# Attention followed by a soft mixture of experts, on one core: five rotating sigmoid buffers, V in three single-buffered tiles, 50 weight units loaded beside attention, and another warm-up

## The chip, the cores and the metric

The kernel runs on one core of a Trainium2 chip. The time is the device time of one execution in microseconds (us); less is better. Before the change the median of three runs is 392.14 us (391.18 to 392.22).

## What is computed

Sigmoid attention (8 batches, 12 heads, 448 tokens, heads of 64), whose output, as 3584 rows of 768, goes through a soft mixture of 8 experts with 4 slots each:

```python
scores = scale * np.matmul(q, k.transpose(0, 1, 3, 2)) - np.log(S)
attn = 1.0 / (1.0 + np.exp(-scores))
x = np.matmul(attn, v)            # then to (N, D) rows
logits = x @ phi
d = softmax(logits, axis=0); slot_input = d.T @ x
slot_out[e] = np.maximum(slot_input[e] @ w1[e], 0.0) @ w2[e]
out = softmax(logits, axis=1) @ slot_out
```

All of it is in float32. The weights w1 and w2 are 48 MB together, more than fits beside the rest.

## The kernel before

**Queues.** The order of the instructions on each engine's queue is the order of the program text; the tile framework adds the waits. All transfers are issued by SP (SyncE), one after the other, and an issue whose destination is not yet free holds up all those behind it.

**Attention.** Two heads make a pair, two pairs (pa, pb) a group, three groups a batch; the loop runs over 24 groups n. A pair's 448 keys are three blocks of 128 and a rest of 64; the rests of the two pairs of a group are worked together as the "middle" block. In a group TensorE does: `qk_full(pa)` and `qk_full(pb)` (L171: scores of three blocks each, in three products with the operands split in two parts by `split`, L150 and L152), `av_full(pa)` and `av_full(pb)` (L189, attention times V), the product with phi for the group before (`logits`, L218; between the two AV halves in the first group of a batch, "edge"), in the second group of a batch ("after") the slot products of the batch before (`slot_mm`, L312, which read the tile y), then `qk_mid(n + 1)` (L182) and `av_mid(n)` (L198). Each block's scores lie in one of four double banks of PSUM (b0 to b3); ScalarE turns them to attention by `sigmoid` (L161). VectorE copies the result out (`evac`, L207), transposes it into y (`turn`), splits the next q and k, adds the logits (L227, L229) and does the softmax steps. The blocks of a group (u = 0 to 5) use the tiles att0 to att4, u = 5 taking att0 again; the middle blocks use attm0 and attm1 in turn.

**Loads beside attention.** In a group SP issues the q and k of the next two pairs (`load_qk`, L135, two buffers), V of the next group (`load_v`, L142, two buffers of 448 KB), and some units of the weights. The weights are 128 units of 384 KB: 64 of w1, then 64 of w2. They go to a ring of 68 tiles: 47 (wa, N_A) that have room from the start and are filled beside attention, and 21 (wb, N_B) that lie where the pools of attention lay. `weights_of` gives 3 units a group in the first batch and then 4, 0 and 3 until N_A are loaded.

**The end of attention.** In group 23 the logits and slots of the last batch follow at once: `last_job` with its own `slot_mm`. After the loop the pools of attention (from q and k to the transposed x) are closed, and the pool wb is opened at the same address; each wb tile waits only for the tiles that lay under it. SP then issues the N_B units, and in the parts `w1_part` (L522), `w2_step` (L588) and `out_batch` (L565, L570, stores at L579) each further unit goes to a ring tile whose weights have been used.

**Start.** SP loads q and k of the first two pairs, V, the constants and phi. TensorE meanwhile runs `WARM` products of 128 x 128 by 128 on zeros (L407), then `qk_mid(0)`.

Of the kernel before, what the change touches and what calls it, by code (L numbers as in the profile page):

```python
# [9 lines left out]
F32 = mybir.dt.float32  # L10
# [6 lines left out]
B, H, S, D = 8, 12, 448, 64  # L17
DM, NSLOT, E, SPE, F = 768, 32, 8, 4, 1024
P = 128
NFULL = 3  # L20
# [4 lines left out]
NFC = F // P  # L25
HALF = DM // 2
UNIT = 768
N_A = 47
N_B = 21
N_LATE = 16  # L30
N_MIX = 4
NATT = 5
QW = 2 * S
NP = B * NPR
NG = B * NQ
WARM = 8
WN = 128
CW = 256
NBK = 4
# [8 lines left out]
def soft_moe_attention(ctx: ExitStack, tc: tile.TileContext, qk, v, phi, w1, w2, cst, out):  # L48
    nc = tc.nc
# [15 lines left out]
    acc = small.tile([P, DM], F32, name="acc")  # L65
# [11 lines left out]
    def ring_tile(dt=F32):  # L77
        n = state["ring"]
        state["ring"] = n + 1
        n %= N_A + N_B  # L80
        if n < N_A:
            return wpa.tile([P, UNIT], dt, name=f"wa{n}")
        return state["wpb"].tile([P, UNIT], dt, name=f"wb{n - N_A}")

    def load_unit():
        n = state["next"]
        if n >= len(units):
            return
        state["next"] = n + 1
        u = units[n]  # L90
        t = ring_tile()[:]
        nc.sync.dma_start(t, w1[u[1:]] if u[0] == "w1" else w2[u[1:]])
        utile[u] = t
# [22 lines left out]
    with ExitStack() as actx:  # L116
        ldq = actx.enter_context(tc.tile_pool(name="ldq", bufs=2))
        sp = actx.enter_context(tc.tile_pool(name="sp", bufs=2))
        ata = actx.enter_context(tc.tile_pool(name="ata", bufs=1))
        atb = actx.enter_context(tc.tile_pool(name="atb", bufs=1))  # L120
        lvp = actx.enter_context(tc.tile_pool(name="lvp", bufs=2))
        yp = actx.enter_context(tc.tile_pool(name="yp", bufs=1))
        xp = actx.enter_context(tc.tile_pool(name="xp", bufs=1))
        bounce = actx.enter_context(tc.tile_pool(name="bounce", bufs=2, space=bass.MemoryType.DRAM))
# [2 lines left out]
        def bank2(i):  # L127
            return ps.tile([P, 2, 512], F32, name=f"b{i}")

        qkts, vs, splits, atts, avs, xTs, ys, dts, drs = {}, {}, {}, {}, {}, {}, {}, {}, {}  # L130

        def load_qk(p):
            if p < NP:
                t = ldq.tile([P, QW], F32, name="qkt")
                nc.sync.dma_start(t[:], qk[p])  # L135
                qkts[p] = t

        def load_v(n):
            if n == NG:
                return  # L140
            vs[n] = lvp.tile([P, 2 * NFULL + 1, P], F32, name="v")
            nc.sync.dma_start(vs[n][:], v[n])  # L142

        def split(p, i, z, copy=nc.vector.tensor_copy):
            w = (S, NQK)[i]
# [11 lines left out]
                    split(p, i, z)  # L157

        def sigmoid(name, sc):
            att = (atb if name == "att0" else ata).tile([P, 2, S], F32, name=name)  # L160
            nc.scalar.activation(att[:], sc[:, :, 0:S], AF.Sigmoid, bias=nbias, scale=QSCALE)  # L161
            return att

        def qk_full(p):
            qs, ks = splits[p, 0], splits[p, 1]
            for c in range(NFULL):
                u = p % 2 * NFULL + c
                sc = bank2(u % 4)
                for z, y in ((0, 0), (0, 1), (1, 0)):
                    for h, r in enumerate(heads):  # L170
                        nc.tensor.matmul(  # L171
                            sc[:, h, 0:S], ks[r, z, c * P:(c + 1) * P], qs[r, y, :], start=(z + y == 0), stop=(z == 1))
                atts[p, c] = sigmoid(f"att{u % NATT}", sc)

        def qk_mid(n):
            if n == NG:
                return
            sc = bank2(3)
            for i, r in enumerate(heads):
                t = qkts[2 * n + i]  # L180
                for h, d in enumerate(heads):
                    nc.tensor.matmul(sc[r, h, 0:S], t[d, S + NQK:QW], t[d, 0:S], start=True, stop=True)  # L182
            atts["mid", n] = sigmoid(f"attm{n % 2}", sc)

        def av_full(p, start, stop):
            n, i = divmod(p, 2)
            for c in range(NFULL):
                for h, r in enumerate(heads):
                    nc.tensor.matmul(  # L189
                        avs["p", p][r, 0:S], vs[n][:, i * (NFULL + 1) + c, r], atts[p, c][:, h, :],  # L190
                        start=(start and c == 0), stop=(stop and c == NFULL - 1))

        def av_mid(n, flags):
            att, vt = atts["mid", n], vs[n]
            for h, d in enumerate(heads):
                for i, r in enumerate(heads):
                    start, stop = flags[i]
                    nc.tensor.matmul(avs["p", 2 * n + i][d, 0:S], vt[r, NFULL, d], att[r, h, :], start=start, stop=stop)  # L198

        def new_x(n):  # L200
            xTs[n] = xp.tile([P, 2, S], F32, name="xT", bufs=2)
# [29 lines left out]
        def logits(n, i):  # L231
            lp = bank2(i)[:, 0, :]
            logits_job(lp, (2 * n, 2 * n + 1))
            return lp
# [161 lines left out]
        def weights_of(n):  # L396
            share = 3 if n < NQ else (4, 0, 3)[n % NQ]
            return max(0, min(share, N_A - state["next"]))

        load_qk(0)  # L400
        load_qk(1)
        load_v(0)
        nc.sync.dma_start(csb[:], cst)
        nc.sync.dma_start(phi_sb, phi)
        pw = bank2(0)[:, 0, :]
        for _ in range(WARM):
            nc.tensor.matmul(pw[:, 0:WN], acc[:, 0:P], acc[:, 0:WN], start=True, stop=True)  # L407
        dmy = ata.tile([P, 2, S], F32, name="attm0")
        nc.scalar.activation(dmy[0:1, 0, 0:1], nbias[0:1, :], AF.Sigmoid)
        split(0, 0, 0)  # L410
        split(0, 1, 0, nc.scalar.copy)
# [5 lines left out]
        for n in range(NG):  # L417
            pa, pb = 2 * n, 2 * n + 1
            bp = n // NQ - 1
            edge, after, third = (n >= NQ and n % NQ == i for i in range(3))  # L420
            final = n == NG - 1
            load_qk(pa + 2)
            load_qk(pb + 2)
            if third:
                slot_evac(bp)
            if n > 0:
                evac(n - 1)
                for p in ((pa - 4, pa - 3) if third else ()) + (() if after else (pa - 2, pa - 1)):
                    turn(p)
            if after:  # L430
                softmax_r(bp)
                softmax_c(bp)
                spread(bp)
            load_v(n + 1)
            for _ in range(weights_of(n)):
                load_unit()
            if third:
                combine_c(bp)
            if edge and bp > 0 or final:
                bq = bp if final else bp - 1  # L440
                combine_d(bq, dts[bq][:, 0, 0:P])
            qk_full(pa)
            split_all(pa + 2)
            qk_full(pb)
            split_all(pb + 2)
            if final:
                avs["p", pa] = bank2(2)[:, 0, :]
                av_full(pa, True, False)
                lg = bank2(0)[:, 0, 0:P]
                nc.tensor.matmul(lg, ident, lt_all[:, B - 1], start=True, stop=False)  # L450
                logits_job(lg, [NP - 4, NP - 3], first=False, last=False)
                avs["p", pb] = bank2(3)[:, 0, :]
                av_mid(n, ((False, True), (True, False)))
                xa = xp.tile([P, 2, S], F32, name="xT", bufs=2)[:, 0, :]
                xTs["p", pa] = xa
                nc.vector.tensor_copy(xa, avs["p", pa][:, 0:S])
                turn(pa)
                av_full(pb, False, True)
                logits_job(lg, [pa], first=False, last=False)
                xb = xp.tile([P, 2, S], F32, name="xT", bufs=2)[:, 0, :]  # L460
                xTs["p", pb] = xb
                nc.scalar.copy(xb[:, 256:S], avs["p", pb][:, 256:S])
                nc.vector.tensor_copy(xb[:, 0:256], avs["p", pb][:, 0:256])
                logits_job(lg, [pb], first=False)
                turn(pb)
                break
            avs[n] = bank2(2)
            for i in range(2):
                avs["p", pa + i] = avs[n][:, i, :]
            av_full(pa, True, False)  # L470
            if edge:
                lp = logits(n - 1, 0)
                logits_add(lp, bp, False)
                softmax_a(bp)
                softmax_b(bp)
            av_full(pb, True, False)
            if n > 0 and not edge:
                lp = logits(n - 1, 3 if after else 0)
                if after:
                    combine_b(bp)  # L480
                logits_add(lp, n // NQ, n % NQ == 1)
            if after:
                slot_job(bp)
            qk_mid(n + 1)
            av_mid(n, ((False, True), (False, True)))
# [7 lines left out]
    for e in range(E):  # L493
        if e < 3:
            if e == 0:
                hacc = small.tile([P, DM], F32, name="acc")
            h = hacc[:, e * 256:(e + 1) * 256]
        elif e < 5:
            h = small.tile([P, 256], F32, name=("phit", "t1")[e - 3])[:]
        else:  # L500
            h = sb2.tile([P, 256], F32, name=f"h{e}", bufs=1)[:]
# [10 lines left out]

    for _ in range(N_B):
        load_unit()
# [151 lines left out]
```

## Time and profile before

| | |
|---|---|
| median of 3 runs | 392.14 us |
| the profiled execution | 390.38 us |
| its span, first to last instruction | 388.6 us |
| TensorE busy (matmuls) | 365.3 us, 94% |
| VectorE, ScalarE busy | 226.1 us, 187.5 us |
| moved by the DMA engines | 97.5 MB, 251 GB/s over the span |
| granted TensorE clock, mean | 0.986 |

The profile comes from one execution. The engines are PE (TensorE matmuls), PEld (its weight loads), DVE (VectorE), ACT (ScalarE), POOL (GpSimd) and SP, whose issues of transfers are called SPq. L with a number is a line of the kernel; a name such as wa or att stands for all tiles of that name. A float32 product is two records on PE. Matmuls overlap one another, so a busy PE says that products are under way, not that the array is full.

### The profile page before, as it was taken

The page shows a single profiled execution, that of the slowest core. Times are in us where ns is not written, and L with a number is a line of the kernel's source. Part 1 is how long each engine was busy: PE and PEld are TensorE (multiplying, and loading weights), DVE is VectorE, ACT ScalarE, POOL GpSimd, SP SyncE. Part 2 cuts the span into 40 slices and gives each one's busy share as a digit, 9 for nine tenths or more (in the row PEclk, how much of TensorE's full clock was granted, in tenths as well). Part 3 has the DMA queues.
Part 4 walks back from the last instruction along what each step waited for, and adds up shares of the span by engine and source line. Part 5 has one row for each costly group of instructions (what it writes and reads, how often), then busy time and mean ns, then how long its engine had stood idle before and what let it go on. Part 6 is the DMA issues. An engine that isn't in the chain of part 4 may idle for free.

```text
span 388.6 us, 9551 instructions
## 1 busy us (share of the span) xinstructions
PE 365.3 (94%) x3994; PEld 189.8 (49%) x3994; DVE 226.1 (58%) x518; ACT 187.5 (48%) x243; POOL 3.3 (1%) x13
## 2 busy tenths in 40 slices
PE   8999999999999999999999999999989989978760
PEld 7444556554555654555554455554455543224220
DVE  3655677775887677697767777776543410430250
ACT  5655676564567556566635666564531110320240
POOL 1000000000000000000000000000020000000000
PEclk9999999999999999999999999999999999999995
DMA  7766855662784567476446654323999999999997
GB/s 228 260 240 236 300 171 183 237 252 83 265 295 138 178 229 255 135 257 240 177 140 228 238 164 156 143 101 98 292 406 400 400 400 400 398 407 399 373 302 231
DMA packets 42363, 97.52 MB, mean 251 GB/s; under 512 B 4816, under 2 KB 16720, under 8 KB 42320
## 3 DMA queue, kind: packets, MB, share of 16 engines
q1 hardware_dynamic: 42320, 96.91, 70.3%
q8 instruction: 31, 0.51, 0.5%
q14 instruction: 12, 0.10, 0.1%
HBM read 85.43 MB, written 11.47 MB: 249 GB/s over the span
## 4 chain that ended last, share of the span: by engine, by line
PE 80%; DMA 14%; DVE 1%; SPq 1%; ACT 1%; issue 0%; ACTq 0%
PE b L189 29%; PE b L171 24%; DMA wa<-in_w_dram 8%; PE b L182 6%; DMA wb<-in_w_dram 6%; PE b L198 5%; PE b L312 4%; PE px L522 4%; PE b L218 3%; PE b L407 1%; PE px L565 1%; PE px L539 1%; SPq L579 1%; DMA out_dram<-wa 1%; DVE wa L570 0%
## 5 line engine op out<-in xcount | busy, mean ns | idle before, releaser
L161 ACT ACTIVATE att<-b,nbias 128x896 f32<-128x896 f32 x144 | 131.9, 1015 | 12.0 <-PE b L171 12.0
L189 PE MATMUL b<-att,v 128*64 128x448 f32 x576 | 115.3, 545 | 0.0
L171 PE MATMUL b<-qs,ks 64*128 64x448 f32 x864 | 95.9, 372 | 0.0
L171 PEld LDWEIGHTS b<-qs,ks 64*128 64x128 f32 x864 | 77.4, 184 | 26.6 <-PE b L182 11.3
L189 PEld LDWEIGHTS b<-att,v 128*64 128x64 f32 x576 | 38.5, 136 | 61.6 <-issue 50.2
L161 ACT ACTIVATE attm<-b,nbias 128x896 f32<-128x896 f32 x24 | 24.2, 1008 | 70.4 <-PE b L182 70.4
L207 DVE COPY xT<-b 128x896 f32<-128x896 f32 x23 | 25.1, 1092 | 32.7 <-PE b L198 32.7
L152 DVE TENSOR_TENSOR qs<-qkt,qs 128x448 fp32r<-128x448 f32 x48 | 30.0, 625 | 1.7
L152 DVE TENSOR_TENSOR ks<-qkt,ks 128x384 fp32r<-128x384 f32 x48 | 26.8, 558 | 1.6
L213 DVE STREAM_TRANSPOSE y<-xT 128x448 f32<-128x448 f32 x48 | 27.3, 617 | 0.4
L182 PE MATMUL b<-qkt 64*64 64x448 f32 x192 | 24.1, 570 | 0.0
L150 DVE CAST qs<-qkt 128x448 fp32r<-128x448 f32 x48 | 18.2, 380 | 8.8 <-DMA qkt<-in_qk_dram 7.7
L198 PE MATMUL b<-attm,v 64*64 64x448 f32 x192 | 22.4, 537 | 0.0
L570 DVE COPY wa<-px 96x768 f32<-96x768 f32 x13 | 12.2, 952 | 13.7 <-PE px L565 12.9
L570 ACT COPY wa<-px 128x768 f32<-128x768 f32 x13 | 10.3, 799 | 18.1 <-PE px L565 14.2
L565 PE MATMUL px<-st,lt_all 32*128 32x384 f32 (+1 forms) x128 | 16.7, 524 | 1.5 <-DVE st L601 0.7
L312 PE MATMUL b<-y,dr 32*32 32x192 f32 x896 | 17.7, 331 | 0.2 <-ACT dr L303 0.2
L218 PEld LDWEIGHTS b<-xT,phit 128*32 128x32 f32 x384 | 9.1, 109 | 17.0 <-issue 13.4
L522 PE MATMUL px<-wa,sT 128*32 128x256 f32 x282 | 16.8, 381 | 0.6 <-DVE sT L380 0.6
L150 DVE CAST ks<-qkt 128x384 fp32r<-128x384 f32 x47 | 16.6, 353 | 0.0
L218 PE MATMUL b<-xT,phit 128*32 128x96 f32 (+1 forms) x384 | 16.0, 266 | 0.2
L601 DVE COPY st<-px 128x384 f32<-128x384 f32 x2 | 1.1, 557 | 25.3 <-PE px L599 25.3
(132 smaller groups left out, 229.3 us busy)
## 6 DMA issues: line engine op xcount, KB each, us to landing
wa<-in_w_dram SPq DMA_DIRECT2D x92, 384.0 KB, 7.7
qkt<-in_qk_dram SPq DMA_DIRECT2D x48, 448.0 KB, 3.8
wb<-in_w_dram SPq DMA_DIRECT2D x36, 384.0 KB, 5.7
v<-in_v_dram SPq DMA_DIRECT2D x24, 448.0 KB, 5.7
out_dram<-wa SPq DMA_DIRECT2D x26, 192.0 KB, 3.3
out_dram<-wa SPq DMA_DIRECT2D x26, 144.0 KB, 3.3
dr<-zd SPq DMA_DIRECT2D x28, 64.0 KB, 2.0
out_dram<-wb SPq DMA_DIRECT2D x6, 192.0 KB, 5.5
```

What stands on the lines that cost most here:

```text
L150: copy(dst[:, 0, :], src)
L152: nc.vector.tensor_tensor(out=dst[:, 1, :], in0=src, in1=dst[:, 0, :].bitcast(F32), op=ALU.subtract)
L161: nc.scalar.activation(att[:], sc[:, :, 0:S], AF.Sigmoid, bias=nbias, scale=QSCALE)
L171: nc.tensor.matmul(sc[:, h, 0:S], ks[r, z, c * P:(c + 1) * P], qs[r, y, :], start=(z + y == 0), stop=(z == 1))
L182: nc.tensor.matmul(sc[r, h, 0:S], t[d, S + NQK:QW], t[d, 0:S], start=True, stop=True)
L189: nc.tensor.matmul(avs["p", p][r, 0:S], vs[n][:, i * (NFULL + 1) + c, r], atts[p, c][:, h, :], start=(start and c == 0), stop=(stop and c ...
L198: nc.tensor.matmul(avs["p", 2 * n + i][d, 0:S], vt[r, NFULL, d], att[r, h, :], start=start, stop=stop)
L207: nc.vector.tensor_copy(xTs[n][:], avs[n][:, :, 0:S])
L213: nc.vector.transpose(ys[b][:, hp, :], xTs["p", p])
L218: nc.tensor.matmul(lp[32 * j:32 * j + 32, 0:TOK[j]], phi_sb[:, p % NPR, :], xTs["p", p][:, TOF[j]:TOF[j] + TOK[j]], start=(first and m == ...
L312: nc.tensor.matmul(sl[a // 2][32 * j:32 * j + 32, a % 2, 0:NPR * BLK], drs[b][32 * a:32 * a + 32, j, c * BLK:(c + 1) * BLK], y[32 * a:32 * ...
L522: nc.tensor.matmul(ph[32 * j:32 * j + 32, uu, 0:256], sT[:, 3 * kh + kc, :], utile[("w1", e, 2 * uu + j // 2, kh)][:, kc * 256:(kc + 1) * ...
```

## The change

The seven sigmoid tiles become five, att0 to att4, each in a pool of its own. They rotate from group to group: after each middle block the list of names is permuted, so that the middle block of the next group stays where it is while the six blocks of the group use the other four. V becomes three tiles with one buffer each: v0 and v1 (192 KB, the three full blocks of either pair) and v2 (64 KB, the middle block), loaded by three transfers at different places of SP's queue. The pools are opened in another order: q and k, their split forms, v0, att4, att3, v2, att0, att1, att2, v1, then y, dr and the transposed x as before. N_A is 50 and N_B 18. The logits of an edge group go to bank 3 instead of bank 0. The warm-up is 37 products of 32 x 32 by 8 columns, on the four diagonal blocks of the array in turn, and three of the old kind.

```diff
-N_A = 47
-N_B = 21
+N_A = 50
+N_B = 18
-NATT = 5
-WARM = 8
+WARM = 3
+FILL = 37
...
-        ata = actx.enter_context(tc.tile_pool(name="ata", bufs=1))
-        atb = actx.enter_context(tc.tile_pool(name="atb", bufs=1))
-        lvp = actx.enter_context(tc.tile_pool(name="lvp", bufs=2))
+        one = {}
+        for name in ("v0", "att4", "att3", "v2", "att0", "att1", "att2", "v1"):
+            one[name] = actx.enter_context(tc.tile_pool(name=f"{name}p", bufs=1))
...
-        def load_v(n):
+        def load_v(n, part):
             if n == NG:
                 return
-            vs[n] = lvp.tile([P, 2 * NFULL + 1, P], F32, name="v")
-            nc.sync.dma_start(vs[n][:], v[n])
+            lo, hi = ((0, NFULL), (NFULL + 1, 2 * NFULL + 1), (NFULL, NFULL + 1))[part]
+            vs[n, part] = one[f"v{part}"].tile([P, hi - lo, P], F32, name=f"v{part}")
+            nc.sync.dma_start(vs[n, part][:], v[n, :, lo * P:hi * P])
...
-            att = (atb if name == "att0" else ata).tile([P, 2, S], F32, name=name)
+            att = one[name].tile([P, 2, S], F32, name=name)
...
+        homes = [f"att{i}" for i in range(5)]
...
-                atts[p, c] = sigmoid(f"att{u % NATT}", sc)
+                atts[p, c] = sigmoid(homes[u % 4], sc)
...
-            atts["mid", n] = sigmoid(f"attm{n % 2}", sc)
+            atts["mid", n] = sigmoid(homes[2], sc)
+            homes[:] = [homes[i] for i in (3, 0, 1, 4, 2)]
...
-        load_v(0)
+        load_v(0, 0)
+        load_v(0, 1)
...
+        for i in range(FILL):
+            r = slice(i % 4 * 32, i % 4 * 32 + 32)
+            nc.tensor.matmul(pw[r, 0:8], acc[r, 0:32], acc[r, 0:8], start=True, stop=True)
...
+            if third:
+                load_v(n, 1)
             load_qk(pa + 2)
             load_qk(pb + 2)
+            load_v(n, 2)
...
-            load_v(n + 1)
             for _ in range(weights_of(n)):
                 load_unit()
+            load_v(n + 1, 0)
+            if not after:
+                load_v(n + 1, 1)
...
-                lp = logits(n - 1, 0)
+                lp = logits(n - 1, 3)
```

The uses of V in `av_full` and `av_mid` follow the new tiles.

## Rows read from the trace of the kernel before

**Rows 1.** Page, part 2: busy tenths in 40 slices of 9.7 us
```profile
PE   8999999999999999999999999999989989978760
DMA  7766855662784567476446654323999999999997
```

**Rows 2.** Page, part 4: share of the chain that ended last, by line
```profile
PE b L189 29%; PE b L171 24%; DMA wa<-in_w_dram 8%; PE b L182 6%; DMA wb<-in_w_dram 6%; PE b L198 5%; PE b L312 4%; PE px L522 4%; PE b L218 3%; PE b L407 1%; PE px L565 1%; PE px L539 1%; SPq L579 1%; DMA out_dram<-wa 1%; DVE wa L570 0%
```

**Rows 3.** The chain in order of time, 268 to 292 us: start, length, what
```profile
274.75 2.41 PE b L189 x12
...
278.15 0.91 PE b L198 x8
279.06 2.43 PE b L189 x12
...
285.43 2.35 PE b L312 x93
```

**Rows 4.** Timeline of SP's issues from 264 and from 287.7 us: start, length, what
```profile
270.11 19.45 SPq L92 DMA_DIRECT2D wb<-in_w_dram  x21
...
287.80 1.75 SPq L92 DMA_DIRECT2D wb<-in_w_dram  x4
```

**Rows 5.** Busy time by stretch: its length, five engines, clock, DMA share, GB/s
```profile
271.00:272.00 1.00, 1.00 (x12) 0.81 (x10) 1.00 (x2) 0.50 (x2) 0.00 (x0) 1.00 0.71 203
...
279.00:280.00 1.00, 1.00 (x10) 0.47 (x8) 0.85 (x2) 0.00 (x0) 0.00 (x0) 1.00 1.15 283
...
288.00:289.20 1.20, 0.94 (x16) 0.29 (x8) 0.58 (x2) 0.24 (x2) 0.87 (x4) 1.00 1.03 407
270.00:289.20 19.20, 18.49 (x268) 10.07 (x260) 10.87 (x28) 10.08 (x16) 1.19 (x5) 1.00 0.90 317
289.20:362.00 72.80, 66.86 (x760) 29.32 (x760) 18.25 (x39) 10.49 (x26) 0.99 (x4) 1.00 1.04 401
```

**Rows 6.** Timeline of DVE, ACT and PE in group 3, 36 to 50 us
```profile
45.30 0.56 DVE L229 TENSOR_TENSOR lt_all<-b,lt_all 64x128 f32<-64x128 f32 x2 [0.41 <-PE b L218]
...
39.27 5.50 ACT L161 ACTIVATE att<-b,nbias 128x896 f32<-128x896 f32 x6 [0.56 <-PE b L171]
...
38.29 3.98 PE L171 MATMUL b<-qs,ks 64*128 64x448 f32 x36
42.20 2.48 PE L189 MATMUL b<-att,v 128*64 128x448 f32 x12
...
45.18 2.48 PE L189 MATMUL b<-att,v 128*64 128x448 f32 x12
47.59 0.98 PE L182 MATMUL b<-qkt 64*64 64x448 f32 x8
...
49.26 1.08 PE L171 MATMUL b<-qs,ks 64*128 64x448 f32 x8
```

**Rows 7.** Timeline of PE at the start, 0 to 12 us
```profile
1.18 3.78 PE L407 MATMUL b<-acc 128*128 128x128 f32 x16 [1.18 <-DVE nbias L69]
4.89 1.49 PE L182 MATMUL b<-qkt 64*64 64x448 f32 x8
6.32 3.92 PE L171 MATMUL b<-qs,ks 64*128 64x448 f32 x36
```

**Rows 8.** Line L365: count, duration in ns (min/median/max), first and last start
```profile
L365 PE MATMUL b<-csb,mrow x8: 165/176/186, 285.0 to 285.1; 1*32 1x1 f32 x8
```

**Rows 9.** Groups of instructions by form: count, busy us, mean ns, idle before
```profile
L407 PE MATMUL b<-acc 128*128 128x128 f32 x16 | 3.8, 431 | 1.2 <-DVE nbias L69 1.2
...
L349 PE MATMUL b<-csb 128*128 128x128 f32 x8 | 1.4, 300 | 0.0
```

**Rows 10.** Page, part 6: issues, count, KB each, median us to landing
```profile
wa<-in_w_dram SPq DMA_DIRECT2D x92, 384.0 KB, 7.7
...
v<-in_v_dram SPq DMA_DIRECT2D x24, 448.0 KB, 5.7
```

**Rows 11.** Tile views: qkt from 0 to 6 us, wb from 270 to 276 us
```profile
L135 SPq DMA_DIRECT2D qkt<-in_qk_dram x2: 396/409/422, 0.7 to 1.2; - x2
...
DMA to landing us min/median/max: 3.2/3.5/3.9
...
DMA to landing us min/median/max: 3.0/3.6/4.8
```

More of the change, by code (lines that the diff above doesn't have):

```diff
@@ L189, in av_full @@
                     nc.tensor.matmul(
-                        avs["p", p][r, 0:S], vs[n][:, i * (NFULL + 1) + c, r], atts[p, c][:, h, :],
+                        avs["p", p][r, 0:S], vs[n, i][:, c, r], atts[p, c][:, h, :],
                         start=(start and c == 0), stop=(stop and c == NFULL - 1))
         def av_mid(n, flags):
-            att, vt = atts["mid", n], vs[n]
+            att, vt = atts["mid", n], vs[n, 2]
             for h, d in enumerate(heads):
@@ L197, in av_mid @@
                     start, stop = flags[i]
-                    nc.tensor.matmul(avs["p", 2 * n + i][d, 0:S], vt[r, NFULL, d], att[r, h, :], start=start, stop=stop)
+                    nc.tensor.matmul(avs["p", 2 * n + i][d, 0:S], vt[r, 0, d], att[r, h, :], start=start, stop=stop)
         def new_x(n):
@@ L405, in soft_moe_attention @@
         pw = bank2(0)[:, 0, :]
+        for i in range(FILL):
+            r = slice(i % 4 * 32, i % 4 * 32 + 32)
+            nc.tensor.matmul(pw[r, 0:8], acc[r, 0:32], acc[r, 0:8], start=True, stop=True)
         for _ in range(WARM):
             nc.tensor.matmul(pw[:, 0:WN], acc[:, 0:P], acc[:, 0:WN], start=True, stop=True)
-        dmy = ata.tile([P, 2, S], F32, name="attm0")
+        dmy = one["att2"].tile([P, 2, S], F32, name="att2")
         nc.scalar.activation(dmy[0:1, 0, 0:1], nbias[0:1, :], AF.Sigmoid)
```

## Prediction

> **What bounds the kernel now.** I read the slices first. TensorE is busy in nine tenths or more of the time from the second slice to about the 28th while the DMA engines are not; from the 29th slice (272 us) the DMA row stands at 9 and the traffic at about 400 GB/s until near the end [rows 1]. So there are two stages: attention, which TensorE sets, and the expert and output stage, which the traffic sets. The chain by line says the same: the attention products L189, L171, L182 and L198 carry 64% of the span, and landings of weights in wa and wb another 14% [rows 2]. Then I read the seam between them, from 268 to 292 us, since whether a weight unit is worth anything is decided there: the chain of the last group, the issues of the SP queue, and the traffic in stretches [rows 3 to 5]. Last come one group of attention [rows 6] and the start [rows 7], because the other parts of the change live there.
>
> The units that go to the space freed by attention (wb) are issued in order by SP, each as the tile under it is released. There are 21; the first goes at 270.11, and the last four, from the 18th on, from 287.80, when the last slot product of L312 has read y at 287.77 [rows 3, 4]. Meanwhile the engines moved on average 317 GB/s from 270 to 289.2 us, 407 GB/s in the last 1.2 us of it, and 401 GB/s from then to 362 [rows 5]. So before, the transfers never run dry once the seam is past.
>
> **Part 1: three more units beside attention (N_A 47 to 50).** Three units of 384 KB (393 kB) leave the stage that the traffic sets: 3 x 393 / 401 = 2.94 us less to move [rows 5, 10]. In attention they go out in groups 18 and 20, where the slices show the DMA engines at 2 to 6 tenths; they cost nothing there.
>
> What gives most of it back is where wb now lies. The attention pools start at the same place relative to wb: qkt 7,168 and qs/ks 13,312 bytes a partition (shapes in the code, 4 bytes an element), 20,480 together. Before, seven sigmoid tiles (25,088) and two V buffers (7,168) follow, so y starts at byte 52,736. A unit takes 3,072 bytes, so wb17 (52,224 to 55,296) is the first over y, and it is indeed the 18th unit that waits for L312 [rows 4]; that checks the layout. After, five sigmoid tiles (17,920) and three V tiles (3,584) follow, so y starts at 41,984 and wb13 (39,936 to 43,008) is the first over it. wb13 to wb17 can be issued only at 287.80. In the last group the sigmoid names have rotated so that the tiles come free in the order in which the new pools lie: wb6 and wb7 after the product of the third block (277.16), wb8 after L198 (279.06), wb9 to wb11 with the products of the last pair (279.9 to 281.2), wb12 after the dummy activation that reads the last sigmoid tile, before 287.80 too [rows 3].
>
> So count units served. Before, up to 289.2: 19.2 us x 317 / 393 = 15.5 units. After, no more than the 13 of wb0 to wb12, because data of wb13 cannot flow until about 1.4 us after its issue: the first unit was issued at 270.11, nothing moved until 271 and 203 GB/s in the next us, half a us at the full rate [rows 4, 5]. 287.80 + 1.4 = 289.2. The engines work through 13 units by about 287 (15.5 less the 2.2 us x 407 / 393 = 2.3 served after that), so they starve for some 2 us. The lag is 2.5 units x 393 / 401 = 2.4 us, against the 2.94 saved. **Net 0.5 us gained.** A restart with one transfer in flight may lose up to 0.2 more; if the later releases of wb6 to wb9 thin the queue, nothing more is lost, as 13 is the ceiling anyway. Bounds: 0.2 to 0.8.
>
> The Trainium skill (SBUF — State Buffer, section The DMA setup-cost knee) puts a fixed cost of about 2 us on every transfer, and calls its own figure too large at middle sizes. The quickest landing of a 384 KB unit here is 3.0 us [rows 11], about what that fit gives (2 + 0.9); but by the rows data flows after 1.4 us. Were the whole 2 us dead, the starving would last 0.6 us longer and the net of this part would be 0.1 us lost instead of 0.5 gained.
>
> **Part 2: five rotating sigmoid buffers.** In a group the fifth sigmoid now waits for the first AV block of the same group, the sixth for the second; before, only the sixth waited, for the first. Queued behind them on ScalarE are the sixth and the middle one. Six sigmoids run from 39.27 to 44.77, spaced 0.9, so the fifth starts at 42.9 and the sixth at 43.8 [rows 6]. The first AV block starts at 42.20 and takes 0.8 (2.48 for three), with its last result at about 43.2, the second at about 44.0. After: fifth at 43.3, sixth at 44.2, ending 45.2. The AV blocks that read them start 0.8 and 1.6 us after 45.18 here (edge group), 0.57 earlier in a group without logits between: 45.4 and 46.2. The cover is 1.0 us on both; cost 0. The logits of an edge group move from bank 0 to bank 3 (bank 0 would now wait for the fifth sigmoid). The middle scores write bank 3 at 47.59, after VectorE has added the logits at 45.30 to 45.86: 1.7 us of cover, cost 0.
>
> **Part 3: V in three single buffers.** V for the next group is loaded at the release by AV, two thirds of a group ahead: v0 is free when the first half of AV ends, 6.4 us after a group starts, and needed 3.9 us into the next; with groups of 10.97 us (38.29 to 49.26) that is 8.5 us for a landing of 5.7 us in the median [rows 6, 10]. v1 is free and needed 2.4 us (one half of AV) later; v2, free at the end of a group, is issued behind the two qkt loads and needed 9.9 us into it. SP waits at these loads, and behind them stand the qkt loads of the next group; those wait anyway for the middle scores, which TensorE runs after the last AV block. Two more issues a group at 0.4 us of SP lie where SP is waiting. Cost 0. The Trainium skill (Trainium Kernel Development and Optimization, Best Practices) says to double-buffer so that transfers overlap compute, and this change does the reverse. By that rule each group would wait for its V; here the wait is covered by 2.8 us.
>
> **Part 4: warm-up.** Before, 16 records of L407 run from 1.18 to 4.9, 431 ns each against 300 for the same shape at L349 [rows 7, 9], so I read them as on the lower of the two clock levels, 1.2 of 2.4 GHz, though the windows print the granted clock of those first us as 1.00. The middle scores follow, 1.49 us against 0.98 later [rows 6, 7]; they need the second qkt as well, issued at 1.2; with the longer of the two landings, 3.9, it comes near 5.1 [rows 11]. After, the nearest row for a tiny product is L365, 32 by 1: 8 records in two rounds of four; the span of 0.1 us between first and last start, the longest reading of the row, makes 13 ns a record at the full level [rows 8]. 74 records are 1.0 us at that, 1.9 at half; at 21 ns, as in L312 (112 records in 2.35 us) [rows 3], 1.6 and 3.1. With six records of 128 columns at 3.71 / 16 = 0.23 (1.4) the warm-up takes 3.3 to 4.5 us, not 3.7. Ending earlier buys nothing, since the second qkt near 5.1 and the slow middle scores set the start of L171 at 6.32; ending 0.8 later costs up to 0.6, as the start of the middle scores moves from 5.1 to 5.7. I take 0, as L365 is the nearer form, with -0.4 (the clock up in time for the second half of the middle scores) to +0.6.
>
> **Sum.** The profiled execution took 390.38 us (span 388.6, 1.8 around it); 390.38 - 0.5 = 389.9. The median of the runs is 1.76 above the profiled one; on it, 392.14 - 0.5 = **391.6**. A measurement here tells 0.3%, 1.2 us, from no change.
>
> **Rivals.** (a) *The transfers don't starve*: the queue at 287.80 is deeper than I count, or y is released earlier. Then the whole 2.94 counts: 389.2. For it: stretches of 200 to 280 GB/s before 280 leave units over [rows 5]. Against: 13 units is a ceiling. Chance 0.28 with the partial forms in which over 1.2 us is kept.
> (b) *The clock rises later*, slower than before: the tiny products, 32 rows by 8 columns each, hold TensorE less busy than 16 full records did, and the scores of group 0 run on the lower level. L171 there takes 3.92 us [rows 7]; wholly at half clock it takes 3.9 more, so 395.5; every us by which the rise comes later costs 0.5. It decides from a rise 3.4 us later (1.7 lost against 0.5 gained). For it: no row here shows such products on a cold clock. Against: they follow one another without a gap. Chance 0.13, typically 393.5.
> (c) *Single buffers stall*: if a group waits 0.1 us for a sigmoid, V or bank 3, 23 groups make 2.3 us: 393.9. Against: 1.0 us of cover or more at each. Chance 0.06.
>
> **Chances and range.** My forecast 0.53, with 390.9 to 392.4 as its own range. Faster by over 0.3%: 0.28 of (a) and 0.03 where the start gains too, 0.31. Slower: 0.13 + 0.06 less 0.02 for weak forms, 0.17. Within: 0.52. The range takes in (a) and the weaker half of (b) and (c): 389.0 to 393.3.
>
> **What would show it.** Right: the 14th wb issue at the end of L312, with no wait before it but the dummy activation; a stretch near 287 to 289 us with little traffic; first wa reuse as before; attention of the same length per group, with the fifth sigmoid waiting for L189. Wrong: traffic at 400 GB/s through 285 to 290 (a); records of L171 in group 0 longer than 370 ns (b); idle TensorE before L189 or L182 in the groups (c).

## The result, and the profile after

The change makes the kernel slower: the median of 15 runs is 394.38 us (392.46 to 395.48), that of 15 runs of the kernel before beside them 392.23 us (390.35 to 394.84). The ratio is 1.0043, with a 95% interval of 1.0024 to 1.0061, so 1.7 us lost (0.9 to 2.4). The forecast was 0.5 us gained. The profiled execution of after took 395.03 us, that of before 390.38; as both lie near the edges of their runs, the pair of traces shows more difference (4.6 us of span) than the medians do (2.2 us). Where the extra lies is told below, at the second trace of before.

The page of after, its slices (now 9.8 us) and the chain by line; the first two answer rows 1, the last rows 2. Lines have moved: L189 is L193, L171 is L174, L182 is L185, L198 is L202, L312 is L316, L161 is L162.

```profile
PE   8999999999999999999999999999999989977760
DMA  7767845773784567477557755443989999999987
GB/s 212 230 245 253 283 144 172 250 251 120 242 290 152 169 231 246 150 242 263 174 156 230 250 164 188 135 148 95 314 314 387 402 401 401 387 366 361 371 296 239
...
PE b L193 28%; PE b L174 23%; DMA wa<-in_w_dram 7%; PE b L185 6%; PE px L535 6%; PE b L202 5%; DMA wb<-in_w_dram 4%; PE b L316 4%; PE b L222 3%; PE px L578 1%; PE px L552 1%; DMA qkt<-in_qk_dram 1%; DMA zd<-t 1%; DVE wa L583 1%; DMA dr<-zd 1%; DMA out_dram<-wa 0%
```

The two stages are as before, but the 30th slice, where before moved 406 GB/s, now stands at 314 like the 29th, and a qkt load and the transfers zd and dr have come into the chain (the softmax weights go to DRAM as zd and come back as dr, the tile that the slot products read beside y).

**The start.** PE at the start of after: start, length, what. It answers rows 7.

```profile
1.18 1.23 PE L413 MATMUL b<-acc 32*32 32x8 f32 x74 [1.18 <-DVE nbias L69]
2.34 1.65 PE L415 MATMUL b<-acc 128*128 128x128 f32 x6
4.27 2.86 PE L185 MATMUL b<-qkt 64*64 64x448 f32 x8 [0.28 <-DMA qkt<-in_qk_dram]
7.06 4.51 PE L174 MATMUL b<-qs,ks 64*128 64x448 f32 x36
```

The 74 thin records are over in 1.23 us, the whole warm-up at 4.0. The middle scores wait 0.28 us for qkt and then take 2.86 us instead of 1.49, the scores of group 0 4.51 us instead of 3.92: TensorE is still on its lower level well into them. Their slowest record takes 740 ns, in before 468, and the median of either is 362. The windows print a granted clock of 1.00 for these first us in every trace here, but only because the clock records of the traces begin later: the first stretch at the full level begins at 5.79 us in before and at 8.39 in after, which is where the records get fast. Group 1 starts at 17.89 in the chain of after and at 16.65 in that of before.

**The seam.** The chain of the last group (answers rows 3), then SP's issues (rows 4), each with start, length and what.

```profile
276.67 2.41 PE b L193 x12
...
280.98 2.43 PE b L193 x12
...
287.34 2.35 PE b L316 x91
```

```profile
272.81 0.33 SPq L143 DMA_DIRECT2D v<-in_v_dram  x1
273.19 19.71 SPq L92 DMA_DIRECT2D wb<-in_w_dram  x18
...
289.72 3.17 SPq L92 DMA_DIRECT2D wb<-in_w_dram  x5
```

The last five of the 18, so from the 14th on, are issued from 289.72, when the last slot product has ended at 289.69. The first goes out behind the load of the last v2, which waited for L202. The traffic by stretch (answers rows 5; the columns are the same, GB/s at the end):

```profile
273.20:287.00 13.80, 13.52 (x125) 7.23 (x122) 8.47 (x21) 8.04 (x12) 0.00 (x0) 1.00 0.89 298
287.00:289.20 2.20, 2.02 (x118) 1.75 (x119) 0.97 (x4) 0.49 (x2) 0.31 (x1) 1.00 1.04 418
289.20:291.20 2.00, 1.66 (x37) 0.56 (x22) 0.85 (x2) 0.65 (x2) 0.95 (x4) 1.00 0.46 122
291.20:299.00 7.80, 7.56 (x126) 4.55 (x130) 2.55 (x9) 0.42 (x2) 0.91 (x4) 1.00 0.97 333
299.00:342.90 43.90, 42.42 (x520) 18.66 (x514) 10.99 (x27) 6.29 (x20) 0.00 (x0) 1.00 1.03 401
```

The queue runs dry for about 2 us, and then for 8 us the engines are busy in 97% of the time and move 333 GB/s instead of 401.

To compare the seam between traces I take one window for each, from 1 us before the scores of the last group (L171 form) start to 26 us after, and divide by a unit: GB/s x 27 / 393. Here before, then after:

```profile
269.76:296.76 27.00, 25.97 (x386) 14.49 (x382) 13.42 (x36) 10.49 (x18) 2.17 (x8) 1.00 0.93 338
```

```profile
271.68:298.68 27.00, 25.97 (x387) 14.50 (x383) 13.41 (x36) 10.60 (x18) 2.17 (x8) 1.00 0.84 287
```

That is 23.2 units against 19.7. After has 3 units less to move and is 3.5 behind.

**Attention.** ACT, PE and DVE in group 3 (answers rows 6):

```profile
40.51 3.70 ACT L162 ACTIVATE att<-b,nbias 128x896 f32<-128x896 f32 x4 [0.50 <-PE b L174]
44.56 1.91 ACT L162 ACTIVATE att<-b,nbias 128x896 f32<-128x896 f32 x2 [0.36 <-PE b L193]
...
39.53 4.02 PE L174 MATMUL b<-qs,ks 64*128 64x448 f32 x36
...
46.47 2.48 PE L193 MATMUL b<-att,v 128*64 128x448 f32 x12
48.87 0.98 PE L185 MATMUL b<-qkt 64*64 64x448 f32 x8
...
50.53 1.75 PE L174 MATMUL b<-qs,ks 64*128 64x448 f32 x14
...
46.83 0.55 DVE L233 TENSOR_TENSOR lt_all<-b,lt_all 64x128 f32<-64x128 f32 x2
```

The fifth sigmoid now waits 0.36 us for the first AV block, and nobody waits for it: the group takes 11.00 us (39.53 to 50.53) where it took 10.97. The logits of bank 3 are added by 47.38, 1.5 us ahead of the middle scores.

### The profile page after: what moved, and what is told of

It reads as the page before. It is cut to its first block, busy times and chain, and to the rows that moved or that the text cites. A ratio compares the mean times of both kernels' runs of the same rounds, so it can differ in the third digit from the quotient of the medians.

```text
span 393.2 us, 9829 instructions
## 1 busy us (share of the span) xinstructions
PE 368.4 (94%) x4058; PEld 189.8 (48%) x4058; DVE 226.4 (58%) x518; ACT 190.3 (48%) x243; POOL 3.3 (1%) x13
## 4 chain that ended last, share of the span: by engine, by line
PE 78%; DMA 15%; DVE 2%; ACT 1%; issue 0%; SPq 0%; ACTq 0%
PE b L193 28%; PE b L174 23%; DMA wa<-in_w_dram 7%; PE b L185 6%; PE px L535 6%; PE b L202 5%; DMA wb<-in_w_dram 4%; PE b L316 4%; PE b L222 3%; PE px L578 1%; PE px L552 1%; DMA qkt<-in_qk_dram 1%; DMA zd<-t 1%; DVE wa L583 1%; DMA dr<-zd 1%; DMA out_dram<-wa 0%
## 5 line engine op out<-in xcount | busy, mean ns | idle before, releaser
L162 ACT ACTIVATE att<-b,nbias 128x896 f32<-128x896 f32 x168 | 158.8, 1007 | 85.2 <-PE b L185 64.7
L193 PE MATMUL b<-att,v 128*64 128x448 f32 x576 | 115.3, 545 | 0.0
L174 PE MATMUL b<-qs,ks 64*128 64x448 f32 x864 | 96.5, 374 | 0.0
L174 PEld LDWEIGHTS b<-qs,ks 64*128 64x128 f32 x864 | 78.0, 186 | 27.0 <-PE b L185 6.3
L193 PEld LDWEIGHTS b<-att,v 128*64 128x64 f32 x576 | 38.5, 136 | 61.5 <-issue 54.1
L185 PE MATMUL b<-qkt 64*64 64x448 f32 x192 | 25.5, 579 | 0.3 <-DMA qkt<-in_qk_dram 0.3
L202 PE MATMUL b<-att,v 64*64 64x448 f32 x192 | 22.4, 537 | 0.0
L316 PE MATMUL b<-y,dr 32*32 32x192 f32 x896 | 18.0, 331 | 0.5 <-DMA dr<-zd 0.4
L535 PE MATMUL px<-wa,sT 128*32 128x256 f32 x300 | 17.8, 381 | 0.6 <-DVE sT L384 0.6
L222 PEld LDWEIGHTS b<-xT,phit 128*32 128x32 f32 x384 | 9.1, 109 | 17.0 <-issue 11.3
L316 PEld LDWEIGHTS b<-y,dr 32*32 32x32 f32 x896 | 12.9, 103 | 4.1 <-issue 2.1
```

Source lines behind the costliest of these rows:

```text
L174: nc.tensor.matmul(sc[:, h, 0:S], ks[r, z, c * P:(c + 1) * P], qs[r, y, :], start=(z + y == 0), stop=(z == 1))
L193: nc.tensor.matmul(avs["p", p][r, 0:S], vs[n, i][:, c, r], atts[p, c][:, h, :], start=(start and c == 0), stop=(stop and c == NFULL - 1))
L202: nc.tensor.matmul(avs["p", 2 * n + i][d, 0:S], vt[r, 0, d], att[r, h, :], start=start, stop=stop)
L222: nc.tensor.matmul(lp[32 * j:32 * j + 32, 0:TOK[j]], phi_sb[:, p % NPR, :], xTs["p", p][:, TOF[j]:TOF[j] + TOK[j]], start=(first and m == ...
L316: nc.tensor.matmul(sl[a // 2][32 * j:32 * j + 32, a % 2, 0:NPR * BLK], drs[b][32 * a:32 * a + 32, j, c * BLK:(c + 1) * BLK], y[32 * a:32 * ...
L535: nc.tensor.matmul(ph[32 * j:32 * j + 32, uu, 0:256], sT[:, 3 * kh + kc, :], utile[("w1", e, 2 * uu + j // 2, kh)][:, kc * 256:(kc + 1) * ...
```

## Experiments

Every ratio is against runs of the kernel before on the same chip; 0.1% is 0.39 us. "Group 1" is the start of its scores in the chain of time, which shows the cost of the start whole; "the seam" is the 27 us window.

**The new warm-up alone, on the kernel before.**

```diff
-WARM = 8
+WARM = 3
+FILL = 37
...
+        for i in range(FILL):
+            r = slice(i % 4 * 32, i % 4 * 32 + 32)
+            nc.tensor.matmul(pw[r, 0:8], acc[r, 0:32], acc[r, 0:8], start=True, stop=True)
```

> The kernel before with only the new warm-up (37 products of 8 columns, three of 128). Theory C (the thin warm-up delays the rise of the TensorE clock, and that is most of the loss): 0.9 to 1.8 us slower than before, and in the profile the scores of group 0 (L171 form) take over 4.2 us against 3.92. Rival T (the loss is in the transfers at and after the seam, the start is chance): within 0.5 us of before. Rival G (the loss is the wait for dr in the first slot job, which comes with the new order of V): within 0.5 us of before.

393.54 us against 392.43; ratio 1.0028 (1.0005 to 1.0051), 1.1 us slower. Its timeline of PE, then group 1 in its chain:

```profile
7.05 3.96 PE L172 MATMUL b<-qs,ks 64*128 64x448 f32 x36
```

```profile
17.39 2.70 PE b L172 x23
```

The loss is theory C's; its mark in the profile isn't. Here the clock was up in time for the scores (at 6.96 us; they took 3.96), and only the middle scores ran slowly (2.87 us). How far the lower level reaches differs between executions (4.63 to 7.14 us in the seven traces with the old warm-up), so single traces do not settle it and the traces of all runs are put together below.

**The changed kernel with the old warm-up.**

```diff
-WARM = 3
-FILL = 37
+WARM = 8
+FILL = 0
```

> The changed kernel with the old warm-up (8 products of 128). Theory C: the loss is gone, -0.5 to +0.5 us against before, since the three units gain next to nothing. Rival T: still 1.2 to 2.2 us slower than before. Rival G: still 0.5 to 1.0 us slower, with the first slot job waiting 0.4 to 0.8 us for dr.

393.27 us against 392.43; ratio 1.0029 (1.0005 to 1.0052), 1.1 us slower. Group 1 starts at 16.92, so the start is as theory C has it, and the first slot product does not wait for dr, so rival G falls, though its time would nearly fit. But theory C's time is missed: the loss isn't gone, and at the seam this kernel moves 288 GB/s, as after does. Part of the loss is rival T's.

```profile
270.72:297.72 27.00, 25.97 (x386) 14.50 (x382) 13.39 (x36) 10.59 (x18) 2.18 (x8) 1.00 0.83 288
```

**47 and 21 units with the new buffers**, first with the new warm-up, then with the old.

```diff
-N_A = 50
-N_B = 18
+N_A = 47
+N_B = 21
```

> The changed kernel with 47 units beside attention and 21 after it; sigmoid and V buffers and warm-up as changed. The wb units then begin at the same place as in the kernel before, and y still starts 10,752 bytes lower, so the 14th to 21st unit wait for the last slot product. Theory C and my account of the seam (13 units is the ceiling until y is read): three units more to move, so 2.4 to 3.0 us slower than the changed kernel, 4 to 5 us slower than before. Rival T (the three units cost as much by the starving as they save, whichever way): within 0.6 us of the changed kernel.

> As the run before it, with the old warm-up too: the new buffers and the new place of V alone. Theory C: 0.9 to 1.8 us faster than the run with the new warm-up and 47 units, 2.4 to 3.0 us slower than before. Rival T: the same as the run with the new warm-up and 47 units within 0.5 us. Rival G: 0.5 to 1.0 us of what is lost stands in the first slot job.

395.97 and 396.54 us against 392.43; ratios 1.0106 (1.0070 to 1.0141) and 1.0107 (1.0075 to 1.0139), 4.2 us slower each. Without the three units the place of y costs all it costs: 293 and 285 GB/s at the seam. That is 3.3 units or some 3.2 us (worked out below), inside both intervals (2.7 to 5.5 us). Between the two the warm-up made no difference that six runs each can show (1.4 us either way); group 1 starts at 18.38 and 17.21, which is theory C's way, but the times do not confirm it here. So the three pairs that differ in the warm-up alone give 1.1, 0.6 (after against the run before this) and 0.0 us for the new one; only the first is clear of the noise.

**No warm-up, on the kernel before.**

```diff
-WARM = 8
+WARM = 0
```

> The kernel before without any warm-up product. Theory C (the clock rises later when the work ahead of the first scores is less, and half of the delay is lost): slower than before by at least what the new warm-up alone cost (1.1 us), up to 2.5 us; in the profile most of the L171 records of group 0 are on the lower level, the stretch over 4.5 us instead of 3.9. Rival S (what the new warm-up costs is chance of the runs): within 0.5 us of before, since the first scores wait for the second qkt anyhow.

395.22 us against 392.78; ratio 1.0052 (1.0030 to 1.0075), 2.0 us slower. PE at its start, then group 1 in its chain:

```profile
4.09 2.81 PE L182 MATMUL b<-qkt 64*64 64x448 f32 x8 [4.09 <-DMA qkt<-in_qk_dram]
6.83 5.21 PE L171 MATMUL b<-qs,ks 64*128 64x448 f32 x36
```

```profile
18.37 1.68 PE b L171 x13
```

The first scores start no later than in after (7.06), since they wait for the second qkt; what is lost is their speed, 5.21 us instead of 3.92; the full level begins at 9.63. Rival S falls.

**Six products of the old kind, on the kernel before.**

```diff
-WARM = 8
+WARM = 6
```

> The kernel before with 6 products of 128 instead of 8: all of the old kind, but over at the time at which the new warm-up is over (3.9 to 4.0 us), with a short wait for qkt behind them. If the new warm-up is slow because its first part is thin (37 products of 32 by 32 by 8): within 0.5 us of before. If because it ends too early and leaves a hole: 0.8 to 1.5 us slower than before, as with the new warm-up.

393.29 us against 392.78; ratio 0.9999 (0.9976 to 1.0022): no change. PE at its start:

```profile
1.18 2.93 PE L407 MATMUL b<-acc 128*128 128x128 f32 x12 [1.18 <-DVE nbias L69]
4.04 2.82 PE L182 MATMUL b<-qkt 64*64 64x448 f32 x8
6.79 3.93 PE L171 MATMUL b<-qs,ks 64*128 64x448 f32 x36
```

This warm-up is over when the new one is (4.1 against 4.0 us), and it costs nothing that the runs can show (0.9 us either way). That speaks for the thin part, but does not settle it. The expected wait for qkt did not come: the middle scores follow at once, where in the three traces with the new warm-up they waited 0.26 to 0.55 us, so the hole was not tried. And the intervals of this run and of the new warm-up alone (0.2 to 2.0) overlap, and so do their traces: the full level begins at 6.44 and 6.96, the middle scores take 2.82 and 2.87 us. Whether the thin products or the wait behind them let the clock rise later stays open.

**y behind the transposed x, 49 units.** From the changed kernel with the old warm-up:

```diff
-N_A = 50
-N_B = 18
+N_A = 49
+N_B = 19
...
-        yp = actx.enter_context(tc.tile_pool(name="yp", bufs=1))
         xp = actx.enter_context(tc.tile_pool(name="xp", bufs=1))
+        yp = actx.enter_context(tc.tile_pool(name="yp", bufs=1))
+        fp = actx.enter_context(tc.tile_pool(name="fp", bufs=1))
...
-            fresh = xp.tile([P, 2, S], F32, name="xT", bufs=2).rearrange("p z n -> p (z n)")[:, 0:DM]
+            fresh = fp.tile([P, DM], F32, name="fresh")
```

> The changed kernel with the old warm-up, 49 units beside attention and 19 after it, and the pools of y and dr moved behind the transposed x, with the tile fresh of the last job in a pool of its own behind them. y then starts at byte 49,152 instead of 41,984 and the 17th unit is the first over it instead of the 14th. Theory T (place of y decides): the 14th to 16th unit are issued by 284.5, traffic does not fall below 300 GB/s between 285 and 297, and two units less than before are moved after attention: 1.0 to 2.0 us faster than before, 2 to 3 us faster than the changed kernel with the old warm-up and 50 units. Rival (restart and y don't matter, the later traffic is what is slow): within 0.7 us of the changed kernel with the old warm-up.

391.69 us against 392.78; ratio 0.9976 (0.9950 to 1.0001), 0.9 us faster; and 2.1 us faster than the changed kernel with the old warm-up by the two ratios. Its traffic by stretch:

```profile
285.00:288.00 3.00, 2.71 (x74) 1.97 (x83) 1.49 (x8) 1.13 (x4) 0.31 (x1) 1.00 1.03 411
288.00:291.00 3.00, 2.60 (x92) 1.44 (x80) 0.98 (x4) 0.65 (x2) 1.02 (x5) 1.00 1.03 410
291.00:297.00 6.00, 5.83 (x99) 3.41 (x100) 1.64 (x7) 0.00 (x0) 0.84 (x4) 1.00 1.03 399
```

The dip is gone, and with it the slow 8 us behind it; 324 GB/s in the 27 us window, 22.3 units where before has 23.2, with two fewer to move. That is theory T; only its time against before falls just short of the forecast, and its interval reaches no change.

**The kernel before once more**, unchanged, for a second trace.

> The kernel before once more, for a second trace of it: 391 to 394 us. If the first trace was an ordinary one: L171 of group 0 starts near 6.3 us and takes 3.9, and traffic between 289 and 362 us is about 400 GB/s. If it was a lucky one, the start is up to 1 us later, or single transfers land 0.6 to 1.1 us late.

393.01 us. Its timeline of PE, its chain and its seam window:

```profile
6.75 3.96 PE L171 MATMUL b<-qs,ks 64*128 64x448 f32 x36
```

```profile
17.09 3.10 PE b L171 x27
...
160.19 3.86 DMA dr<-zd
```

```profile
271.71:298.71 27.00, 25.97 (x386) 14.48 (x382) 13.39 (x36) 10.48 (x18) 2.17 (x8) 1.00 0.92 337
```

The first trace was a lucky one: this one is 2.6 us longer (span 391.2 against 388.6). It starts group 1 0.4 us later and loses 1.5 us more up to the last group's scores: 0.4 in a group that waits for a late dr, which the first trace never did, and 1.1 in one whose middle scores pause (from 200.6 us) without a wait that the profile shows. The rest, 0.7, comes after. The seam is the same, 337 GB/s. So waits for dr are no mark of the changed kernel, as rival G had it, and of the 4.6 us between the first two traces over 2 belong to chance.

Some 2 us of the 4.6 lie in a place that the prediction did not look at, late in the stage that the traffic sets. From 60 to 95 us behind the start of the last group's scores, before, this trace and after moved

```profile
330.76:365.76 35.00, 29.16 (x208) 9.72 (x204) 8.33 (x10) 6.86 (x9) 0.00 (x0) 1.00 1.04 399
```

```profile
332.71:367.71 35.00, 28.81 (x202) 9.28 (x194) 7.80 (x9) 6.87 (x9) 0.00 (x0) 1.00 1.03 387
```

```profile
332.68:367.68 35.00, 29.51 (x201) 9.27 (x200) 8.19 (x9) 6.61 (x9) 0.00 (x0) 1.00 1.02 375
```

24 GB/s over 35 us are 2.1 units. The new warm-up alone and the six products on the kernel before have 380 there too, and the other three traces with the new pools 379 to 383. So most of it comes and goes without the change; whether the change adds to it, these traces cannot tell, and its cause stays open.

**50 units, y behind the transposed x, v2 a group ahead.** As the run before last, with:

```diff
-N_A = 49
-N_B = 19
+N_A = 50
+N_B = 18
...
-            one[name] = actx.enter_context(tc.tile_pool(name=f"{name}p", bufs=1))
+            one[name] = actx.enter_context(tc.tile_pool(name=f"{name}p", bufs=2 if name == "v2" else 1))
...
-        fp = actx.enter_context(tc.tile_pool(name="fp", bufs=1))
...
-            fresh = fp.tile([P, DM], F32, name="fresh")
+            fresh = yp.tile([P, DM], F32, name="dr")
...
+        load_v(0, 2)
...
-            load_v(n, 2)
...
+            load_v(n + 1, 2)
             for _ in range(weights_of(n)):
```

> The changed kernel with the old warm-up, 50 units beside attention, y and dr behind the transposed x, the tile fresh in the place of dr, and v2 with two buffers, loaded a group ahead (so that the first wb issue no longer stands behind a wait for L202). y starts at byte 49,664; the 17th unit is the first over it. Theory T (what counts is how many units can be issued before y is read, and how many are left): three units less to move than before (2.9 us), of which 0.4 to 0.9 us goes to a later filling of the queue: 1.6 to 2.6 us faster than before. Rival (whatever is saved at the seam is lost again later, or in attention): less than 1.0 us faster.

391.71 us against 391.90; ratio 0.9987 (0.9956 to 1.0018), 0.5 us faster at the middle, which this measurement cannot tell from no change. That is less than theory T's range and within the rival's. The seam window:

```profile
271.27:298.27 27.00, 25.80 (x386) 14.38 (x382) 13.38 (x36) 10.58 (x18) 2.11 (x8) 1.00 0.90 318
```

21.8 units, 1.4 fewer than before, so 1.6 of the 3 units should be left. That 1.6 us isn't seen in the times; their interval just reaches it. Part of it may be lost in the late stretch, as the rival has it: this trace moved 371 GB/s there, the one with 49 units too. One trace each does not show it, and what became of the 1.6 us stays open. Neither this version nor the one with 49 units is shown to beat the kernel before by a margin clear of the noise.

**y first, on the kernel before.**

```diff
+        yp = actx.enter_context(tc.tile_pool(name="yp", bufs=1))
         ata = actx.enter_context(tc.tile_pool(name="ata", bufs=1))
...
-        yp = actx.enter_context(tc.tile_pool(name="yp", bufs=1))
```

> The kernel before with nothing but the pool of y and dr moved ahead of the sigmoid tiles: y starts at byte 20,480, the 7th unit is the first over it, and the 7th to 21st wait for the last slot product. Theory T: at most 6 units are served where the first trace of before had 15.5 at 289.2, so 9.5 units x 0.98 = 9.3 us slower, and 10 to 11 us if the restart is as slow as in the changed kernel (1.3 units). Rival (the place of y is of no account): within 1 us of before.

403.53 us against 391.90; ratio 1.0296 (1.0243 to 1.0349), 11.6 us slower. Its traffic by stretch:

```profile
282.00:285.00 3.00, 2.72 (x26) 1.05 (x22) 1.52 (x5) 2.12 (x5) 0.00 (x0) 1.00 0.02 5
285.00:288.00 3.00, 2.82 (x99) 2.29 (x104) 1.44 (x6) 0.81 (x4) 0.31 (x1) 1.00 0.00 0
288.00:291.00 3.00, 2.42 (x74) 1.28 (x67) 1.33 (x4) 0.65 (x2) 1.36 (x6) 1.00 0.35 76
291.00:294.00 3.00, 3.00 (x54) 1.80 (x50) 0.48 (x4) 0.00 (x0) 0.50 (x2) 1.00 0.78 255
294.00:297.00 3.00, 3.00 (x52) 1.72 (x44) 0.75 (x1) 0.00 (x0) 0.00 (x0) 1.00 0.94 324
```

Six units, then nothing until y is read, then again a slow return. The seam window has 173 GB/s, 11.9 units: 11.3 behind before, times 0.98 us is 11.1 of the 11.6. Nothing else was changed, so the place of y alone does this.

## Why the prediction was wrong

**The start (part 4): a term taken as 0 that costs about 0.9 us.** The start of group 1 in the chains, with 8 products of the old kind, is 16.65, 16.92, 17.21, 16.79, 17.09, 17.38 and 17.16 (seven traces, mean 17.03), 17.13 with 6; with the new warm-up 17.89, 17.39 and 18.38 (mean 17.89); with none 18.37. So the new warm-up gives back most of what a warm-up brings. The new warm-up alone cost 1.1 us (0.2 to 2.0), none at all 2.0, six full products nothing that shows. The clock records say the same: the full level begins at 4.63 to 7.14 us in the seven traces (mean 6.0), at 6.96, 8.39 and 9.08 with the new warm-up (mean 8.1), at 9.63 with none.

Only the length of the warm-up had been priced, and that was too long: 3.3 to 4.5 us forecast, 2.8 measured (1.18 to 3.99), since the thin records took 1.2 us where 1.9 to 3.1 had been put for the lower level. What failed is the step from "it ends early enough" to "nothing is lost". Part 4 had the start of the scores set by the second qkt near 5.1 and by middle scores as slow as before; but in after the middle scores, started at 4.27, ran wholly on the lower level, 2.86 us instead of 1.49, and the scores began at 7.06 instead of 6.32. Whether the warm-up brings the clock up was put into rival (b) at a chance of 0.13, on the ground that the records follow one another without a gap. They do, and the clock rose later all the same; the thin products or the wait behind them, no run separates. The price was right: 2.1 us later at half of each us make 1.05, against 0.9 measured.

**The seam (part 1): the mechanism right, one term too small.** The count of 13 units that can be issued before y is read, the 14th issue at the end of the slot product, the idle 2 us and its place are as forecast. Mis-sized was the restart, "up to 0.2 more" us: 7.8 us at 333 instead of 401 GB/s are 1.3 units. The lag itself was somewhat less than forecast: up to 291.2 after had moved 13.4 units by its rows, before 15.5 up to the same place, 2.1 behind instead of 2.5. Over four traces with the new pools (287, 288, 293, 285 GB/s) and four with the old (338, 337, 338, 334) the seam costs 3.3 units, not 2.5, against 3 saved: 0.3 us lost instead of 0.5 gained. The fixed cost of about 2 us of the Trainium skill (SBUF — State Buffer, section The DMA setup-cost knee) would have given 0.1 us lost, nearer to the result; but not for its reason: traffic was back at 249 GB/s from 291 to 292, that is from 1.3 to 2.3 us after the issue at 289.72, and what was missing then was the rate.

**Sum.** 0.9 + 0.3 = 1.2 us slower, inside the measured 0.9 to 2.4. The rest, up to the middle of 1.7, is not assigned; nor is it in the changed kernel with the old warm-up, where the seam's 0.3 stands against 1.1 (0.2 to 2.0).

**Buffers (parts 2 and 3): right.** The fifth sigmoid starts 5.03 us after the group (44.56 - 39.53), against 5.0 forecast (43.3 - 38.3), and hides as forecast. Single-buffered V delays no AV block: from the start of group 1 to that of the last scores it is 254.5 to 254.8 us in the four traces with the new buffers and 47 or 50 units, and 254.0 to 256.3 in the six with the old, with groups of 10.8 to 13.0 us but for single ones in traces of either kind (14.6 at most). So the rule of the Trainium skill (Trainium Kernel Development and Optimization, Best Practices) to double-buffer is not borne out here, where a load has 8.5 us. Overlooked were the things queued behind these loads on SP: the first wb issue now stands behind the last v2 and comes 0.5 us after the scores of group 23 start instead of 0.65 before; that costs nothing only because 13 units are the ceiling anyway. In group 4 of after, zd landed 3.4 us after its issue, and most of the first slot products waited for dr until 60.59, as its chain has it; that group took 0.6 us longer than the others of its place in a batch:

```profile
53.52 3.41 DMA zd<-t
...
57.80 2.66 DMA dr<-zd
...
60.59 1.43 PE b L316 x56
```

With the old buffers such waits come too, at other batches (the second trace of before, and the run without a warm-up), so I book nothing for it.

**Rivals.** (a), that the transfers don't starve, is wrong. (b), that the clock rises later, is what happened, at about 0.9 us. (c), stalls of single buffers, did not happen.

## What to carry to other kernels

Memory that was taken from pools that come free early and given to tiles that are filled early brought nothing here: the room that the first loads after a stage can use is what lies ahead of the tile that is released last, and that tile belongs at the end of the region. A transfer stage that runs dry can pay twice, as here: some 2 units for the idle time and 1.3 for the return to its rate. A warm-up of TensorE is worth what it does to the records behind it: read the length of the first real products, in several traces, before counting the instructions as a saving.

## What had not been expected of the hardware

- 37 products of 32 by 32 by 8 on four diagonal blocks run at 1.23 us for 74 records, 17 ns a record, on the lower clock level, about as fast as the nearest forms ran at the full level (13 to 21 ns). With them ahead of three products of 128 columns the full level began at 6.96 to 9.08 us in three traces; with six such products, over at the same time, at 6.44 in the one trace there is.
- After an idle queue the 16 DMA engines were busy in 97% of the time and yet moved 333 GB/s for 8 us, then 401 (at 103%); after the long pause with y first it was 255 and 324 GB/s in the two stretches of 3 us behind it. Fewer units were in flight than later, so this may in part be a thin queue; no run here separates it.
- Executions of one kernel differ by up to 4.5 us (before, 390.35 to 394.84). In the two traces of before, 2.6 us apart, it is small things that move about: the clock rises at 5.79 or 6.67 us, a dr transfer lands late, the middle scores of one group pause, and traffic late in the kernel is 399 or 387 GB/s.
